# Hash-masked attention, rational feed-forward and mixture of experts in one kernel: one PSUM tile for a head's projection sums, the row-sum constant on GpSimd, and two weight conversions placed at the head of the feed-forward

## The chip, the cores and the metric

The kernel runs on one core of one Trainium2 chip. The metric is device time in microseconds (us), the median of several runs. Beside it one execution was profiled; its trace gives the rows shown below. Engines are named as in the trace: PE is TensorE's matmuls, PEld its weight loads, DVE is VectorE, ACT is ScalarE, POOL is GpSimd, SP is SyncE, which here only issues DMAs.

## The reference

Three layers follow one another. Only the first two are touched by the change.

```python
# attention: batch 2, 8 heads, 768 positions, head size 64, 6 hash bits
q_bits = (einsum('bhsd,dk->bhsk', q, proj) > 0)          # the same for k
mask   = q_bucket[:, :, :, None] == k_bucket[:, :, None, :]
scores = where(mask, q @ k.T / 8, -1e9);  scores -= scores.max(-1)
attn   = exp(scores);  attn = attn / (attn.sum(-1) + 1e-9);  x = attn @ v
# feed-forward on 1536 tokens of 512: w_in 512 x 2048, w_out 2048 x 512
h = x @ w_in
g = (a0 + a1*h + a2*h**2 + a3*h**3) / (1 + |b0|*|h| + |b1|*h**2 + 1e-6)
x = g @ w_out
# mixture of experts on the result: 8 experts, softmax gate with 8 rounds of balancing
```

The two feed-forward matrices come as 64-bit floats, everything else as 32-bit floats.

## The kernel before, in words

**Attention.** There are 16 heads. A head is worked in three groups of two 128-row tiles of queries, so the main loop runs over 48 groups (`it`), with lags: while group `it` gets its scores, group `it-2` is transposed and group `it-3` is multiplied with v. `scores` (L270 on) multiplies into a two-bank PSUM tile `s` of 768 columns; a DVE instruction (L285) copies it to the SBUF tile `e` and takes the row's minimum, and ACT (L286) writes the exponential over `e` and the row's sum into column 0 of a pair in `rse`, a tile whose column 1 was set to 1e-9 before the loop. `norm` reduces each pair with a DVE instruction (L291), takes the reciprocal on DVE (L292), and has POOL scale the two `e` tiles (L294). `trans` transposes `e` on PE (L308), ACT copies the high part (`pth`, L106) and DVE takes the low part (`ptl`, L109). `values` multiplies on PE (L323).

`prep_head_a` and `prep_head_b` make a head's operands two groups ahead of its use. `prep_head_b` (L251 on) multiplies q and k by the hash projection: for columns 0 to 511 and then 512 to 767 four matmuls sum into a PSUM bank `hp` (L259), and a DVE instruction (L260) thresholds each into `bits`; SP then issues two DMAs (L262, L263) that copy rows of `bits` into the score operands. PSUM's eight banks are four single banks (tag `b`: `tp`, `hp`, `pt`, `av`) and two two-bank tiles (tag `s`: `s`).

**Weights.** A 64-bit block of a feed-forward weight (128x512 values) is made into a high and a low 32-bit part by `prep_weights`, in five steps: an absolute value on ACT (L169) and a clamp on POOL (L170); four DVE instructions on the bits (L180 to L183); an add on POOL (L186), behind which the next raw block is loaded; a copy to the high part on ACT (L106, tile `wa` or `wb`); the low part on POOL (L103). Two tiles `c` are shared by all conversions. Eight blocks, 0 to 3 of w_in (`wa`) and of w_out (`wb`), are converted in the attention, each further one in the feed-forward, where the DVE steps write to a PSUM bank `bits`.

**Feed-forward.** Its steps run over 4 quarters of the hidden size, 3 tiles of 512 tokens and 4 blocks (48 steps). A step has 12 matmuls of the first product (`h`, L354), the rational function (ACT L372 to L374, POOL L375, DVE L376 and L377; one step later ACT L380 and L381, DVE L382 to L384; then ACT `gh` and POOL `gl`), and six steps later 12 matmuls of the second product (`acca`, L405).

**Order.** In the attention the order of the instructions on each engine is a planner's: it simulates the program with its own costs and takes ready work by its place in the program. It moves work far ahead: the eight conversions, written at groups 35 to 44, stand in the trace from 11 us on. In the feed-forward and behind it PE, ACT, DVE and POOL issue in the order in which the code is written; where the first of these instructions fall among those of the attention is the planner's too. Each engine runs its queue in order.

The lines around the change are L251 to L294 and the loop's `if it in wprep`; the feed-forward's loop begins with empty lists of conversions under way:

Of the kernel before, what the change touches and what calls it, by code (L numbers as in the profile page):

```python
# [14 lines left out]
F32 = mybir.dt.float32  # L15
# [5 lines left out]
AF = mybir.ActivationFunctionType  # L21
ALU = mybir.AluOpType
AX = mybir.AxisListType
# [3 lines left out]
QROW, KROW = 64, 96  # L27
# [8 lines left out]
def kernel(  # L36
# [16 lines left out]
    pe, act, dve, pool, sp = nc.tensor, nc.scalar, nc.vector, nc.gpsimd, nc.sync  # L53

    B, H, S, D = q.shape
    NB = proj.shape[1]
    DM, FF = moe_w_in.shape
    E, _, F2 = w1.shape
    P = 128
# [29 lines left out]
    def bank(name):  # L89
        return ps.tile([P, 512], F32, tag="b", bufs=4, name=name)  # L90

    def two_banks(name):
        return ps_s.tile([P, 2, 512], F32, tag="s", bufs=2, name=name)
# [19 lines left out]
    ap = qkv_pool_stack.enter_context(tc.tile_pool(name="attn", bufs=2))  # L113
# [137 lines left out]
    def prep_head_b(i):  # L251


        a1, a2, b1_, b2, _ = st[i]
        bits = ap.tile([P, S], F32R, tag="bits", bufs=1, name="bits")
        for n0, n1 in COLS:
            hp = bank("hp")[0:KROW + 2 * NB, 0:n1 - n0]
            for m, (j, r) in enumerate(((0, a1), (1, a1), (2, b1_), (3, b1_))):
                pe.matmul(hp, lhsT=pjr[:, j, 0:KROW + 2 * NB], rhs=r[:, n0:n1], start=m == 0, stop=m == 3)  # L259
            dve.tensor_scalar(bits[QROW:KROW + 2 * NB, n0:n1], hp[QROW:], thr[QROW:KROW + 2 * NB, 0:1],  # L260
                              thr[QROW:KROW + 2 * NB, 1:2], ALU.is_ge, ALU.mult)
        sp.dma_start(a2[QROW:QROW + 2 * NB].bitcast(F32), bits[QROW:QROW + 2 * NB].bitcast(F32))  # L262
        sp.dma_start(b2[QROW:QROW + 2 * NB].bitcast(F32), bits[KROW:KROW + 2 * NB].bitcast(F32))  # L263

    es = {}
    rsum_eps = [ap.tile([P, 2, 2], F32, tag=f"rse{n}", bufs=1, name="rse") for n in range(4)]
    for t in rsum_eps:
        dve.memset(t, 1e-9)

    def scores(gi, j):  # L270
        i, g = divmod(gi, G)
        a1, a2, b1_, b2, _ = st[i]
        t = 2 * g + j
        s = two_banks("s").rearrange("p a n -> p (a n)")
        cs = slice(t * P, (t + 1) * P)
        for n0, n1 in COLS:
            pe.matmul(s[:, n0:n1], lhsT=a1[:, cs], rhs=b1_[:, n0:n1], start=True, stop=False)
            pe.matmul(s[:, n0:n1], lhsT=a2[0:QROW + 2 * NB, cs], rhs=b2[0:QROW + 2 * NB, n0:n1],  # L278
                      start=False, stop=True)
        nm = ap.tile([P, 1], F32, tag="nm", bufs=4, name="nm")  # L280
        if j == 0:
            es[gi] = ([ap.tile([P, S], F32, tag="e", bufs=EB, name="e") for _ in range(2)],
                      rsum_eps[gi % len(rsum_eps)])
        e, rs = es[gi]
        dve.tensor_scalar(e[j], s[:, 0:S], BIG, None, ALU.min, ALU.min, accum_out=nm)  # L285
        act.activation(e[j], e[j], AF.Exp, bias=nm, scale=-1.0, accum_out=rs[:, j, 0:1])  # L286

    def norm(gi):
        e, rs_eps = es[gi]
        rs = ap.tile([P, 2], F32, tag="rs", bufs=4, name="rs")  # L290
        dve.tensor_reduce(rs, rs_eps, AX.X, ALU.add)  # L291
        dve.reciprocal(rs, rs)  # L292
        for j in range(2):
            pool.tensor_scalar(e[j], e[j], rs[:, j:j + 1], 0.0, ALU.mult, ALU.add)  # L294
# [403 lines left out]
    pjr = ap.tile([P, 4, P], F32R, tag="pjr", bufs=1, name="pjr")  # L698
# [8 lines left out]
    thr = const.tile([P, 2], F32, name="thr")  # L707
# [6 lines left out]
    dve.tensor_tensor(thr[:, 0:1], thr[:, 0:1], rowf[:, 2:3], ALU.add)  # L714

    prep_head_b(0)

    wprep = {NG - 13 + 3 * j: j for j in range(QF)}
    bits_in_psum = False
    for it in range(NG + VLAG):  # L720
        if it == CONST_AT:
            ca = const.tile([P, 4], F32, name="ca")
            cb = const.tile([P, 2], F32, name="cb")
            sp.dma_start(ca, moe_a.partition_broadcast(P))
            sp.dma_start(cb, moe_b.partition_broadcast(P))
            wg = const.tile([P, KC, E], F32, name="wg")
            sp.dma_start(wg, w_gate.rearrange("(c p) e -> p c e", p=P))
            wg2 = const.tile([P, KC, 2 * E], F32R, name="wg2")
            dve.tensor_copy(wg2[:, :, 0:E], wg)
            dve_lo(wg2[:, :, E:2 * E], wg, wg2[:, :, 0:E])  # L730

            ab = const.tile([P, 2], F32, name="ab")
            dve.tensor_scalar(ab, cb, -1.0, None, ALU.mult)
            dve.tensor_tensor(ab, ab, cb, ALU.max)
            na = const.tile([P, 4], F32, name="na")
            dve.tensor_scalar(na, ca, -1.0, None, ALU.mult)
            dbias = const.tile([P, 1], F32, name="dbias")
            dve.memset(dbias, 1.0 + 1e-6)
        if it == WLOAD:
            for c in range(2):  # L740
                load_weights(0, c)
                load_weights(1, c)
        i, g = divmod(it, G)
        ti, vi = it - TLAG, it - VLAG
        if it < NG:
            scores(it, 0)
        if i + 1 < len(heads) and g < 2:
            (prep_head_a, prep_head_b)[g](i + 1)
        if 0 <= ti < NG:
            trans(ti, 0)  # L750
        if 0 <= vi < NG:
            values(vi)
        if it < NG:
            scores(it, 1)
        if 0 <= ti < NG:
            trans(ti, 1)
            trans(ti, 2)
        if it < NG:
            norm(it)
        if it in wprep:  # L760
            for m in range(2):
                list(prep_weights(m, wprep[it]))
    qkv_pool_stack.close()

# [34 lines left out]
    def go(gen):  # L799

        return next(gen, 0) is None

    narrowing, acting, summing = [], [], []
    with tc.manual_schedule(engines={mybir.EngineType.PE, mybir.EngineType.Activation, mybir.EngineType.DVE,
                                     mybir.EngineType.Pool}):
        ws = None
        late, xs = None, [None] * 3
        for s in range(NS + QF):  # L810
            n = s - NS
            if n < 0:
                new = step_a(*divmod(s, QF))
            u, j = divmod(s - ALAG - QF, QF)
            summed = []
            if 0 <= u < NU - 1:
                gemm2_a(u, j)
                summed = [(u, j)]
            elif u == NU - 1:

                for j in range(3):
                    gemm2_a(u, j, range(QF - 1))
                for j in range(3):
                    gemm2_a(u, j, range(QF - 1, QF))
                summed = [(u, j) for j in range(3)]
            old_w = narrowing
            for w in old_w:
                go(w)
            for w in acting:
                go(w)  # L830
            if n < 0:
                go(new)
            narrowing = [prep_weights(m, i) for m, i in preps.get(s, ())]
            narrowing = [w for w in narrowing if go(w)]
            for w in old_w:
                go(w)
            for w in acting:
                go(w)
            for w in old_w:
                go(w)  # L840
            for w in narrowing:
                go(w)
            last = n >= 0 and summed[0][0] == NU - 1
            if last:
                gemm2_a(NU - 1, 3)
                for k in range(3):
                    go(xgen)
            for k in summed:
                sum_a(*k)
            if last:  # L850
                go(xgen)
                sum_a(NU - 1, 3)
                go(xgen)
                go(xgen)
            acting = [new] if n < 0 else []

            if s == NS - QS + ALAG + 1:
                def stemp():
                    c = [conv.tile([P, 512], F32, tag="c", name="c").rearrange("p (k c f) -> p k c f", k=2, c=2)
                         for _ in range(2)]  # L860
                    return c[0][:, 0], c[0][:, 1], c[1][:, 0]
                ws = w_blocks(0, stemp)
            if ws is not None and s < NS and not go(ws):
                if s == NS - 2:
                    wsec = w_second(0)
                go(wsec)
            if n == 0:
                x_stack.close()
                xs[0] = ffn_pool("x0", 1)
                xs[2] = ffn_pool("xt", 1)  # L870
                xgen = x_blocks(0)
                go(xgen)
            if last:
                break
# [77 lines left out]
```

## Time and profile before

| what | value |
|---|---|
| median of 3 runs | 1589.35 us (1587.63 to 1591.01) |
| profiled execution, whole | 1589.4 us |
| its span, first to last instruction | 1587.6 us |
| granted TensorE clock, mean | 0.994 |
| PE matmul busy | 1536.8 us (97%) |
| DVE busy | 1199.3 us (76%) |
| POOL busy | 938.9 us (59%) |
| ACT busy | 622.1 us (39%) |

The time of the whole is 1.8 us more than the span. In the trace the attention ends at about 291 us, the feed-forward at about 575 us, and the rest is the mixture of experts. The share of busy time of an engine is a mean over these stages, which have different limits.

### The profile page before, as it was taken

What the parts mean: (1) busy time and instruction counts of PE and PEld (TensorE: products, weight loads), DVE (VectorE), ACT (ScalarE), POOL (GpSimd) and SP (SyncE); (2) the same over time, 40 slices, a digit from 0 to 9 for tenths busy, and PEclk for the clock granted to TensorE, in tenths of its full rate; (3) what the DMA queues carried; (4) which work ended last, traced back from release to release, by engine and by line L of the source; (5) the groups of instructions that cost most, each with busy time, mean ns of one, the idle gap of its engine ahead of it and who ended that gap; (6) DMA issues with size and microseconds to landing.
All of it is one profiled execution on the core that took longest, in us unless ns stands there. A gap on an engine that the chain in (4) does not pass through costs nothing.

```text
span 1587.6 us, 22241 instructions
## 1 busy us (share of the span) xinstructions
PE 1536.8 (97%) x8071; PEld 1355.8 (85%) x8071; DVE 1199.3 (76%) x2116; ACT 622.1 (39%) x1167; POOL 938.9 (59%) x1165
## 2 busy tenths in 40 slices
PE   5989999899999999999999999999999999999999
PEld 4888889687777877889899999989899998989898
DVE  7989999799999984886666766676666666666665
ACT  4878888788777842111111111111111111111111
POOL 6777875577777976456644653564465356436530
PEclk8999999999999999999999999999999999999999
DMA  5322221021212000101010110101011001101002
GB/s 170 86 83 79 81 70 25 14 67 54 66 53 67 14 27 27 41 27 40 27 41 27 41 40 27 36 32 40 27 40 41 27 28 40 40 27 40 14 1 80
DMA packets 49406, 71.85 MB, mean 45 GB/s; under 512 B 4368, under 2 KB 35088, under 8 KB 49296
## 3 DMA queue, kind: packets, MB, share of 16 engines
q1 hardware_dynamic: 48432, 68.85, 14.1%
q8 instruction: 64, 1.05, 0.3%
q10 hardware_dynamic: 864, 1.57, 0.3%
q14 instruction: 46, 0.38, 0.1%
HBM read 59.79 MB, written 3.15 MB: 40 GB/s over the span
## 4 chain that ended last, share of the span: by engine, by line
PE 65%; DVE 2%; ACT 0%; issue 0%; DVEq 0%; ACTq 0%
PE accb L599 33%; PE prod L534 29%; PE acca L405 2%; PE h L354 1%; PE lp L635 0%; DVE t L470 0%; DVE t L473 0%; DVE c L559 0%; DVE part L417 0%; DVE gl L555 0%; ACT xb L106 0%; DVE t L480 0%; ACT gh L554 0%; DVE t L484 0%; DVE csum L676 0%
## 5 line engine op out<-in xcount | busy, mean ns | idle before, releaser
L534 PE MATMUL prod<-xb,ww 128*128 128x384 f32 x2688 | 481.7, 336 | 1.8 <-ACT m L106 1.3
L599 PE MATMUL accb<-wb,gh 128*128 128x512 f32 x1536 | 475.7, 391 | 2.9 <-ACT osum L106 2.5
L534 PEld LDWEIGHTS prod<-xb,ww 128*128 128x128 f32 x2688 | 469.8, 188 | 8.0 <-ACT m L106 1.6
L610 DVE SCALAR_TENSOR_TENSOR osum<-accb,gp,osum 128x512 f32<-128x512 f32 x336 | 251.7, 749 | 127.7 <-PE accb L599 126.0
L599 PEld LDWEIGHTS accb<-wb,gh 128*128 128x128 f32 x1536 | 287.0, 188 | 60.9 <-ACT osum L106 2.9
L599 PE MATMUL accb<-wb,gl 128*128 128x512 f32 x768 | 300.9, 392 | 0.4 <-DVE gl L555 0.4
L100 POOL TENSOR_SCALAR wb<-rb 128x512 fp32r<-128x512 f32 x64 | 40.2, 627 | 405.8 <-PE accb L599 405.8
L554 ACT ACTIVATE gh<-c 128x384 fp32r<-128x384 f32 x256 | 134.3, 526 | 352.5 <-DVE c L559 352.1
L106 ACT ACTIVATE m<-prod 128x384 f32<-128x384 f32 x64 | 31.5, 492 | 457.9 <-PE prod L534 457.9
L599 PEld LDWEIGHTS accb<-wb,gl 128*128 128x128 f32 x768 | 144.2, 188 | 32.0 <-DVE gl L555 1.7
L555 DVE SCALAR_TENSOR_TENSOR gl<-c,gh 128x384 fp32r<-128x384 f32 x256 | 165.2, 645 | 1.3 <-ACT gh L554 0.9
L559 DVE TENSOR_TENSOR c<-prod,u 128x384 f32<-128x384 f32 x192 | 106.6, 558 | 61.7 <-PE prod L534 54.1
L354 PE MATMUL h<-xh,wa 128*128 128x512 f32 x384 | 126.7, 392 | 3.4 <-DVE tu L377 3.4
L405 PE MATMUL acca<-gh,wb 128*128 128x512 f32 x384 | 126.4, 391 | 2.8 <-DVE part L417 1.7
L109 DVE TENSOR_TENSOR ptl<-pt,pth 128x512 fp32r<-128x512 f32 x144 | 94.5, 682 | 19.1 <-ACT pth L106 18.3
L559 DVE TENSOR_TENSOR c<-prod,m 128x384 f32<-128x384 f32 x64 | 35.7, 558 | 92.4 <-PE prod L534 92.4
L103 POOL TENSOR_TENSOR ww<-ra,ww 128x256 fp32r<-128x256 f32 x128 | 95.4, 746 | 10.7
L294 POOL TENSOR_SCALAR e<-e,rs 128x768 f32<-128x768 f32 x96 | 88.8, 937 | 20.8 <-DVE rs L292 11.3
L308 PE MATMUL pt<-idr,e 128*128 128x128 f32 x576 | 83.0, 279 | 11.1 <-DVE ptl L109 4.9
L285 DVE TENSOR_SCALAR_CACHE_REDUCE e<-s 128x768 f32<-128x768 f32 x96 | 90.9, 949 | 2.1 <-PE s L278 1.7
L286 ACT ACTIVATE e<-e,nm 128x768 f32<-128x768 f32 x96 | 89.9, 936 | 3.8 <-DVE e L285 3.1
L354 PEld LDWEIGHTS h<-xh,wa 128*128 128x128 f32 x384 | 72.1, 188 | 22.4 <-DVE tu L377 5.9
(168 smaller groups left out, 2546.3 us busy)
## 6 DMA issues: line engine op xcount, KB each, us to landing
ra<-in_moe_w_dram SPq DMA_DIRECT2D x32, 512.0 KB
rb<-in_moe_w_dram SPq DMA_DIRECT2D x32, 512.0 KB
ra<-in_moe_w_in_dram SPq DMA_DIRECT2D x16, 512.0 KB
rb<-in_moe_w_out_dram SPq DMA_DIRECT2D x16, 512.0 KB
qkv<-in_q_dram SPq DMA_DIRECT2D x16, 192.0 KB
qkv<-in_k_dram SPq DMA_DIRECT2D x16, 192.0 KB
qkv<-in_v_dram SPq DMA_DIRECT2D x16, 192.0 KB
a<-a SPq DMA_DIRECT2D x16, 192.0 KB
```

Source lines behind the costliest of these rows:

```text
L103: pool.tensor_tensor(lo, src, hi.bitcast(F32), ALU.subtract)
L109: dve.tensor_tensor(lo, src, hi.bitcast(F32), ALU.subtract)
L285: dve.tensor_scalar(e[j], s[:, 0:S], BIG, None, ALU.min, ALU.min, accum_out=nm)
L286: act.activation(e[j], e[j], AF.Exp, bias=nm, scale=-1.0, accum_out=rs[:, j, 0:1])
L354: pe.matmul(hps, lhsT=a[:, c], rhs=x[:, c], start=m == 0, stop=m == 3 * KC - 1)
L405: pe.matmul(o, lhsT=l[:, js], rhs=r, start=f == 0 and m == 0, stop=f == QF - 1 and m == 2)
L534: pe.matmul(o, lhsT=w[:, i, c], rhs=x[:, j, c], start=n == 0, stop=n == 5)
L554: act.activation(gh, c, AF.Relu)
L555: low.append(lambda: dve.scalar_tensor_tensor(gl, c, 0.0, gh.bitcast(F32), ALU.max, ALU.subtract))
L559: dve.tensor_tensor(c, o, x, ALU.add)
L599: pe.matmul(o, lhsT=l[:, ts], rhs=r, start=n == 0 and m == 0, stop=n == 1 and m == 2)
L610: dve.scalar_tensor_tensor(d, o, gate["p"][:, n, e:e + 1], d, ALU.mult, ALU.add)
```

## The change

The four single-bank accumulations of a head's projections become one two-bank tile of tag `s`, thresholded by one DVE instruction over 768 columns. The pairs with 1e-9 and the reduction over them go; POOL adds 1e-9 to the two row sums, and the reciprocal stays on DVE. Blocks 2 and 3 of w_out are no longer converted in the attention: their conversions are the first work written in the feed-forward's loop, with their first two steps ahead of step 0 and the others inside it.

```diff
         bits = ap.tile([P, S], F32R, tag="bits", bufs=1, name="bits")
+        rows = slice(QROW, KROW + 2 * NB)
+        hp = two_banks("hp").rearrange("p a n -> p (a n)")
         for n0, n1 in COLS:
-            hp = bank("hp")[0:KROW + 2 * NB, 0:n1 - n0]
             for m, (j, r) in enumerate(((0, a1), (1, a1), (2, b1_), (3, b1_))):
-                pe.matmul(hp, lhsT=pjr[:, j, 0:KROW + 2 * NB], rhs=r[:, n0:n1], start=m == 0, stop=m == 3)
-            dve.tensor_scalar(bits[QROW:KROW + 2 * NB, n0:n1], hp[QROW:], thr[QROW:KROW + 2 * NB, 0:1],
-                              thr[QROW:KROW + 2 * NB, 1:2], ALU.is_ge, ALU.mult)
+                pe.matmul(hp[0:KROW + 2 * NB, n0:n1], lhsT=pjr[:, j, 0:KROW + 2 * NB], rhs=r[:, n0:n1],
+                          start=m == 0, stop=m == 3)
+        dve.tensor_scalar(bits[rows], hp[rows, 0:S], thr[rows, 0:1], thr[rows, 1:2], ALU.is_ge, ALU.mult)
...
-    rsum_eps = [ap.tile([P, 2, 2], F32, tag=f"rse{n}", bufs=1, name="rse") for n in range(4)]
-    for t in rsum_eps:
-        dve.memset(t, 1e-9)
...
-                      rsum_eps[gi % len(rsum_eps)])
+                      ap.tile([P, 2], F32, tag="rsum", bufs=4, name="rsum"))
...
-        act.activation(e[j], e[j], AF.Exp, bias=nm, scale=-1.0, accum_out=rs[:, j, 0:1])
+        act.activation(e[j], e[j], AF.Exp, bias=nm, scale=-1.0, accum_out=rs[:, j:j + 1])
...
-        dve.tensor_reduce(rs, rs_eps, AX.X, ALU.add)
+        pool.tensor_scalar(rs, rsum, 1e-9, None, ALU.add)
         dve.reciprocal(rs, rs)
...
         if it in wprep:
-            for m in range(2):
+            for m in range(2 if wprep[it] < 2 else 1):
                 list(prep_weights(m, wprep[it]))
...
-    narrowing, acting, summing = [], [], []
+    narrowing, acting, summing = [prep_weights(1, i) for i in (2, 3)], [], []
...
+        for w in narrowing + narrowing:
+            go(w)
         for s in range(NS + QF):
```

## Rows read from the trace of the kernel before

**Rows 1.** Stretches of the run: length, then busy us (instructions) of each engine.
```profile
core 0: us, PE busy (x) PEld busy (x) DVE busy (x) ACT busy (x) POOL busy (x), PEclk, DMA share, GB/s
95.10:232.00 136.90, 127.38 (x930) 115.48 (x928) 124.11 (x271) 110.31 (x233) 108.71 (x133) 0.99 0.28 78
223.20:269.30 46.10, 45.95 (x349) 42.06 (x348) 42.06 (x96) 39.70 (x85) 31.84 (x43) 1.00 0.16 40
310.00:515.00 205.00, 195.64 (x838) 155.35 (x838) 193.95 (x291) 164.60 (x269) 155.88 (x141) 1.00 0.20 62
```
**Rows 2.** Waits from 223.2 to 269.3 us: total us, times, longest.
```profile
PEld pt L308 <- issue: 1.0, 3, 0.4
PEld pt L308 <- POOL e L294: 0.7, 2, 0.4
```
**Rows 3.** Order of time on SP: start, us; one such DMA ends each head's preparation.
```profile
95.10 0.75 SPq L263 DMA_DIRECT2D b<-bits  x1
...
166.84 0.76 SPq L263 DMA_DIRECT2D b<-bits  x1
...
231.99 0.76 SPq L263 DMA_DIRECT2D b<-bits  x1
...
262.66 0.77 SPq L263 DMA_DIRECT2D b<-bits  x1
```
**Rows 4.** Waits from 95.1 to 232 us.
```profile
ACT wa L106 <- POOL c L186: 5.0, 2, 2.5
ACT wb L106 <- POOL c L186: 4.8, 2, 2.5
```
**Rows 5.** Order of time at a conversion's end, with idle time before in brackets.
```profile
212.91 1.04 POOL L186 TENSOR_TENSOR c<-rb 128x512 f32<-128x512 f32 x1
...
213.98 0.63 ACT L106 ACTIVATE wb<-c 128x512 fp32r<-128x512 f32 x1 [2.29 <-POOL c L186]
...
217.79 0.31 PEld L308 LDWEIGHTS pt<-idr,e 128*128 128x128 f32 x3 [0.74 <-POOL e L294]
```
**Rows 6.** Instruction groups of DVE, 95.1 to 232 us: count, busy us, mean ns, idle before.
```profile
L260 DVE TENSOR_SCALAR bits<-hp,thr 44x512 fp32r<-44x512 f32 x8 | 6.6, 820 | 0.3
L260 DVE TENSOR_SCALAR bits<-hp,thr 44x256 fp32r<-44x256 f32 x8 | 4.4, 556 | 0.0
...
L291 DVE TENSOR_REDUCE rs<-rse 128x2 f32<-128x4 f32 x24 | 3.5, 148 | 0.5 <-ACT e L286 0.4
```
**Rows 7.** Order of time around a head's projections.
```profile
227.15 0.29 PEld L259 LDWEIGHTS hp<-a,pjr 128*108 128x108 f32 x2
...
228.44 0.08 DVE L285 DVE_READ_ACCUMULATOR e<-s 128x1 f32 x1
...
228.54 0.19 PEld L277 LDWEIGHTS s<-b,a 128*128 128x128 f32 x1
...
229.83 1.29 DVE L260 TENSOR_SCALAR bits<-hp,thr 44x512 fp32r<-44x512 f32 x2
```
**Rows 8.** Instruction groups of POOL: the smallest, and the smallest scaling.
```profile
L702 POOL IOTA row<- 128x1 int32 x1 | 0.1, 128 | 0.0
...
L100 POOL TENSOR_SCALAR xh<-xp 128x256 fp32r<-128x256 f32 x12 | 5.0, 420 | 5.4 <-DVE xp L334 5.4
```
**Rows 9.** Order of time at the attention's end and the feed-forward's start.
```profile
284.97 0.14 PEld L308 LDWEIGHTS pt<-idr,e 128*128 128x128 f32 x1 [1.32 <-POOL e L294]
...
291.64 0.74 POOL L103 TENSOR_TENSOR xl<-xp,xh 128x256 fp32r<-128x256 f32 x1
...
294.52 1.29 POOL L375 TENSOR_TENSOR tq<-tq,tw 128x512 f32<-128x512 f32 x1 [2.15 <-ACT tq L373]
295.14 0.69 DVE L376 TENSOR_TENSOR tu<-tu,h 128x512 f32<-128x512 f32 x1 [4.08 <-ACT tu L374]
295.85 0.69 ACT L380 ACTIVATE tr<-tq,dbias 128x512 f32<-128x512 f32 x1 [0.74 <-POOL tq L375]
```
**Rows 10.** Instruction groups of DVE, 310 to 515 us: one of a conversion's four steps.
```profile
L180 DVE TENSOR_SCALAR bits<-c 128x512 int32<-128x512 int32 x23 | 15.8, 689 | 0.0
```

More of the change, by code (lines that the diff above doesn't have):

```diff
@@ L282, in scores @@
             es[gi] = ([ap.tile([P, S], F32, tag="e", bufs=EB, name="e") for _ in range(2)],
-                      rsum_eps[gi % len(rsum_eps)])
+                      ap.tile([P, 2], F32, tag="rsum", bufs=4, name="rsum"))
         e, rs = es[gi]
         dve.tensor_scalar(e[j], s[:, 0:S], BIG, None, ALU.min, ALU.min, accum_out=nm)
-        act.activation(e[j], e[j], AF.Exp, bias=nm, scale=-1.0, accum_out=rs[:, j, 0:1])
+        act.activation(e[j], e[j], AF.Exp, bias=nm, scale=-1.0, accum_out=rs[:, j:j + 1])
     def norm(gi):
-        e, rs_eps = es[gi]
+        e, rsum = es[gi]
         rs = ap.tile([P, 2], F32, tag="rs", bufs=4, name="rs")
-        dve.tensor_reduce(rs, rs_eps, AX.X, ALU.add)
+        pool.tensor_scalar(rs, rsum, 1e-9, None, ALU.add)
         dve.reciprocal(rs, rs)
```

## The prediction

> **What bounds the kernel now.** I read the stretches of the run first, since each stage has another limit [rows 1]. From 223.2 to 269.3 us, three heads of attention without a weight conversion, PE is busy 45.95 of 46.10 us and DVE 42.06. From 95.1 to 232 us, heads with conversions among them, PE is busy only 127.38 of 136.90 while DVE has 124.11. In the feed-forward (310 to 515 us) DVE has 193.95 of 205 and PE 195.64: neither has room to catch up. The mixture of experts behind it is untouched.
>
> The second view is the order of time on SP: the last DMA of each head's preparation marks the heads [rows 3]. From 231.99 to 262.66 us two heads take 30.67 us, 15.34 each. From 95.10 to 231.99 eight heads take 136.89 us, 14.2 more than 8 x 15.34 = 122.7. The granted clock of 0.99 there [rows 1] explains about 1% of 136.9, 1.4 us; 12.8 us are left for the conversions that fall there, four whole ones and the end of a fifth.
>
> The third view, the waits of that stretch, says how a conversion costs this [rows 4]: ACT stood at the copy to `wa` or `wb` four times, 9.8 us in all, for POOL's add. ACT's queue is in order, so the copies of transposed tiles and the exponentials behind it wait too. One case in order of time [rows 5]: POOL adds at 212.91, ACT has waited 2.29 us when its copy starts at 213.98, and at 217.79, a scaling later, PE waits 0.74 us for POOL's `e`.
>
> **The change part by part.** All against the profiled execution: 1589.4 us, of which 1587.6 is its span; it equals the median of the runs, 1589.35, to 0.1 us.
>
> *Two conversions leave the attention.* By the ACT waits one costs 9.8 / 4 = 2.45 us [rows 4]. By the heads it is 12.8 / 4 = 3.2 at most, and by the last two alone, from 166.84 to 231.99 us (65.15 us for four heads, less 61.36), 1.9 [rows 3]. I take 2.45, the value in the middle: -4.9 us. The bounds are 0, if the planner, which sets this order anew, makes the remaining conversions stand as badly in the room that is left, and -6.4. Their absolute values and clamps need only raw data and a tile `c`, so the planner can still move them into gaps of the attention; no engine waits in order behind another for these, and I count them at nothing.
>
> *They stand at the head of the feed-forward.* There POOL has, in order, two adds (L186), then L375 of step 0; the second add needs all eight DVE steps. These take 0.689 us each in the feed-forward [rows 10], 5.5 us. DVE is free from 291.06 (L376 starts at 295.14 after 4.08 idle) [rows 9]. So if the front part was done earlier: DVE is through at 296.6, the second add (1.04, rows 5) ends at 297.6, L375 (1.29) at 298.9, where it ended at 295.81 before. ACT's L380 of step 0 follows it [rows 9]: +3.1 us. DVE's idle 4.08 us hide most of the eight steps; what shows is their end and the adds in POOL's queue. The delay stays, since the next steps hang on the same chain and the 205 us behind it are 95% full on both engines [rows 1]. If the planner lets nothing start before the attention's last POOL work ends at 292.38 (291.64 + 0.74), a clamp comes ahead (estimate 0.7 us, between the 0.42 for 256 columns in rows 8 and the 1.04 of the add in rows 5), so DVE starts at 293.1, 2.0 later: +5.1. If the DVE steps fit into the last microseconds of the attention, 0. The loads of blocks 4 and 5 of w_out move with the adds, to about 297 us, off SP's queue in the attention; that queue is free then. They are first needed at step 6; six steps of 12 matmuls lie between: covered.
>
> *One threshold instruction.* 820 + 556 ns become, with the slope (820 - 556) / 256 = 1.03 ns a column, 820 + 264 = 1084 ns: 0.29 us of DVE a head [rows 6]. With the reduction, 3 x 0.148 us a head, DVE gets 0.74 us a head back. Beside a PE that is busy 99.7% [rows 1] I cost this at nothing.
>
> *Two banks from the scores.* `hp` now takes one of the two score tiles from its first weight load at 227.15 to the threshold's end, 229.83 + 1.29 = 231.12: 4.0 us [rows 7]. The score that began at 228.54 would need the other tile, whose reading ended at 228.52: it just fits. So there is no stall with this order; if DVE is late by some tenths, the score waits as long. Queued behind a late score on PE are transposes and v products, which the planner may put first. Bounds 0 and 0.5 us x 16 heads = +8; I take +0.5, near the row that shows a fit.
>
> *The add on POOL.* The trace has no POOL add of two columns. Below it stands the 0.128 us of a one-column instruction, above it 0.420 for 256 columns [rows 8]; I take 0.2. POOL is busy 31.84 of 46.10 us [rows 1], so its time is covered. What is new is a wait: DVE's reciprocal now waits for POOL, and behind it on DVE stand score reads and `ptl`, for which PE waits. With two groups between scaling and transposing this is hidden, except at the attention's end, where PE waits 1.32 us for the scaling [rows 9]: the longer chain adds 0.2 and a hand-over, +0.3. Bounds 0 and the +8 of the third rival.
>
> Sum: -4.9 + 3.1 + 0.5 + 0.3 = -1.0, so 1588.4 us.
>
> **A rule weighed.** The waits of PE in the stretch without conversions are 1.0 + 0.7 = 1.7 us of 46.10 in their two largest groups [rows 2], and PEld is busy 42.06 [rows 1]. The Trainium skill's page "Perfetto Trace Analysis", section "Identifying the Most-Contended Engine", says that the matmuls' busy share is no good measure of PE's headroom and the weight loads' busy share is. By it PE has 9% left there where the matmul row shows 0.3%, and the DVE relief would pay. By the matmul row the relief is worth 0, by the rule something up to those waits; this is the first rival.
>
> **The rivals.**
> First, faster: the DVE relief pays. PE's waits of 1.7 us in three heads [rows 2] are 0.57 us a head; over some 15 heads 8.5 us, of which the relief of 0.74 us a head might take half: -4.3 more, 1584.1 us. For it: 0.7 us of them stand behind POOL's scaling, which waits for DVE's reciprocal. Against it: the larger part is put down to no wait, and 0.3% idle matmul time leaves no place for it.
>
> Second, slower: nothing is won in the attention. The planner's new order lets the six conversions left, or a late score, cost what the eight did; then 3.1 + 0.5 + 0.3 stay: 1593.3 us. It decides once the attention's end comes less than 0.7 us earlier. For it: these stalls come from an order planned with costs that the chip does not keep. Against it: each of the four ACT waits belongs to one conversion.
>
> Third, slower: DVE waits for POOL. In a head without conversions DVE has (46.10 - 42.06) / 3 = 1.35 us idle, with the 0.74 won 2.1, or 0.7 for each of its three pairs. If the reciprocal waits longer than that for a POOL that is in a scaling, DVE becomes the bound; 0.85 us a pair would add 0.15 x 48 = 7 us: 1595.6 us. For it: POOL's queue is in order too. Against it: the planner sees the dependency and can put the reciprocal later.
>
> Fourth, the two conversions do not leave: the planner, free to place the first feed-forward work, moves most of it back into the attention. Then little changes: 1589.5 us.
>
> **How the numbers follow.** The forecast has 0.40 (its own range 1585 to 1592), the first rival 0.28, the second 0.16, the third 0.10, the fourth 0.06. A measurement of this kernel tells about 0.2% from no change, 3.2 us. Faster by more: 0.28 and 0.06 from the forecast's lower end, 0.34. Slower: 0.16 + 0.10, and 0.01 of the forecast, 0.27. Within: 0.39. The range reaches from beyond the first rival to the third, 1581 to 1596 us.
>
> **What would show it.** ACT's waits for POOL's add in the attention fall by about two, and the last third of the heads runs at 15.3 us. The attention ends 3 to 5 us earlier; L380 of step 0 then starts 8 us after the last `xp`, where it was 5. If heads without conversions take less than 15.2 us, the first rival holds; if they take 15.8 or more with DVE idle before L292, the third; with PE idle before the scores, the shared tiles cost. An attention that ends as late as before would make the forecast wrong.

## The result and the profile after

The changed kernel takes 1606.67 us (median of 5 runs, 1605.96 to 1607.88), against 1589.75 us for the kernel before in the same comparison: ratio 1.0107, 95% interval 1.0093 to 1.0122. It is 17 us slower; the forecast was 1588.4 us with a range up to 1596. The profiled span went from 1587.6 to 1604.3 us, 16.7 more. The last `xp` (the sum of a head's two value halves on DVE, which ends the attention) starts at 304.14 us where it was 290.64, 13.5 later, and the first ACT L380 of the feed-forward (now L378) at 312.64, where it was 295.85 [rows 9]: 16.8 later. In the kernel before and in the changed kernel:

```profile
290.64 0.42 DVE L334 TENSOR_TENSOR xp<-av,avt 64x256 f32<-64x256 f32 x1 [1.01 <-ACT avt L106]
```

```profile
304.14 0.42 DVE L332 TENSOR_TENSOR xp<-av,avt 64x256 f32<-64x256 f32 x1 [1.01 <-ACT avt L106]
...
312.64 0.69 ACT L378 ACTIVATE tr<-tq,dbias 128x512 f32<-128x512 f32 x1 [0.62 <-POOL tq L373]
```

So the loss is in the attention, with 3.3 us more at the head of the feed-forward, and what follows takes as long as before. The profiled execution of a later run, `e6_dve_add`, took 5368.6 us against some 1589 in its other nine, so that run is judged by its times alone.

The stretches again, four heads of attention without a conversion (length, then busy us of each engine):

```profile
core 0: us, PE busy (x) PEld busy (x) DVE busy (x) ACT busy (x) POOL busy (x), PEclk, DMA share, GB/s
171.77:239.76 67.99, 65.60 (x465) 57.77 (x464) 54.97 (x113) 53.22 (x112) 48.82 (x73) 1.00 0.24 64
```

They answer to the second row of [rows 1]: there PE was busy 45.95 of 46.10 us (99.7%), here 65.60 of 67.99 (96.5%), at a granted clock of 1.00 in both. DVE went from 91% to 81%: it has less to do, and yet the heads take longer. The heads, by the DMA that ends each preparation (start, us):

```profile
173.71 0.77 SPq L264 DMA_DIRECT2D b<-bits  x1
191.28 0.77 SPq L264 DMA_DIRECT2D b<-bits  x1
207.70 0.77 SPq L264 DMA_DIRECT2D b<-bits  x1
225.27 0.77 SPq L264 DMA_DIRECT2D b<-bits  x1
241.70 0.77 SPq L264 DMA_DIRECT2D b<-bits  x1
```

Heads alternate between 17.6 and 16.4 us, 17.0 on average, where heads without conversions took 15.34 [rows 3]. The waits of the same stretch (total us, times, longest):

```profile
DVE rs L290 <- POOL rs L289: 7.5, 10, 2.5
POOL rs L289 <- ACT e L284: 7.4, 6, 2.4
ACT e L284 <- DVE e L283: 7.0, 10, 2.2
```

None of the first two kinds could exist before: DVE now stands at the reciprocal for POOL's add, and POOL stands at the add for ACT's row sum. From 60 to 290 us:

```profile
POOL rs L289 <- ACT e L284: 25.7, 20, 2.4
DVE rs L290 <- POOL rs L289: 25.6, 33, 2.7
PEld pt L306 <- POOL e L292: 2.5, 4, 0.7
```

Seven of the 33 waits of DVE are longer than 1.6 us and make 16.4 of the 25.6 us. One of the long cases in order of time, with the idle time before an instruction in brackets:

```profile
213.49 1.28 DVE L109 TENSOR_TENSOR ptl<-pt,pth 128x512 fp32r<-128x512 f32 x2
...
214.52 0.18 ACT L284 ACTIVATION_READ_ACCUMULATOR e<-e,nm 128x1 f32 x1
...
215.34 0.50 POOL L100 TENSOR_SCALAR sq<-qkv 128x384 fp32r<-128x384 f32 x1
...
215.93 1.01 POOL L103 TENSOR_TENSOR sq<-qkv,sq 128x384 fp32r<-128x384 f32 x1
...
217.03 0.21 POOL L289 TENSOR_SCALAR rs<-rsum 128x2 f32<-128x2 f32 x1
217.27 0.17 DVE L290 RECIPROCAL rs<-rs 128x2 f32<-128x2 f32 x1 [2.50 <-POOL rs L289]
217.37 0.96 DVE L283 TENSOR_SCALAR_CACHE_REDUCE e<-s 128x768 f32<-128x768 f32 x1
...
218.39 0.19 PEld L275 LDWEIGHTS s<-b,a 128*128 128x128 f32 x1 [0.36 <-DVE e L283]
218.43 0.94 ACT L284 ACTIVATE e<-e,nm 128x768 f32<-128x768 f32 x1 [2.22 <-POOL e L292]
```

DVE is free at 214.77, and ACT has made the row sum by 214.70 (214.52 + 0.18). DVE's next instruction is the reciprocal, and POOL's add, which could have run then, stands behind the split of the next head's q. DVE waits 2.50 us for an instruction of 0.21. Behind the reciprocal stands the reading of a score tile; ACT's exponential has waited 2.22 us when it starts and PE's next score 0.36 for the tile.

The planner also orders DVE otherwise than before. From 60 to 290 us, 33 of the 40 reciprocals in the changed kernel's trace stand directly ahead of a score reading; before it was 4 of 42, and 28 stood directly behind one. So a wait at the reciprocal now falls on the score readings.

### The profile page after: what moved, and what is told of

Its sections match the earlier page's. It is cut to its first block, busy times and chain, and to the rows that moved or that the text cites. A ratio compares the mean times of both kernels' runs of the same rounds, so it can differ in the third digit from the quotient of the medians.

```text
span 1604.3 us, 22263 instructions
## 1 busy us (share of the span) xinstructions
PE 1549.2 (97%) x8071; PEld 1360.1 (85%) x8071; DVE 1193.6 (74%) x2048; ACT 624.3 (39%) x1167; POOL 948.0 (59%) x1213
## 4 chain that ended last, share of the span: by engine, by line
PE 64%; DVE 2%; ACT 0%; issue 0%; DVEq 0%; ACTq 0%
PE accb L597 32%; PE prod L532 28%; PE acca L403 2%; PE h L352 1%; PE lp L633 0%; DVE t L468 0%; DVE t L471 0%; DVE c L557 0%; DVE part L415 0%; DVE gl L553 0%; ACT xb L106 0%; DVE t L478 0%; ACT gh L552 0%; DVE t L482 0%; DVE csum L674 0%
## 5 line engine op out<-in xcount | busy, mean ns | idle before, releaser
L403 PEld LDWEIGHTS acca<-gh,wb 128*128 128x128 f32 x384 | 72.1, 188 | 20.3 <-DVE part L415 2.5
```

Of the source, the lines that this page charges most:

```text
L403: pe.matmul(o, lhsT=l[:, js], rhs=r, start=f == 0 and m == 0, stop=f == QF - 1 and m == 2)
```

## The experiments

The theories: **A**, DVE's in-order queue stands at the reciprocal for POOL's add, which is late because of what POOL does before it (the third rival); **B**, the two-bank tile takes a score tile and PE waits; **C**, any new order of the planner costs this; **D**, the chain from the exponential to the scaling is longer, on whatever engine; **E**, POOL's own time and queue. Ratios are to the kernel before, measured beside each.

**One part at a time.** `e1_two_bank` has only the first hunk of the diff, `e2_pool_add` only the row-sum hunks, `e3_conv_moved` only the last three; `e4_no_pool_add` is the changed kernel without the row-sum hunks.

> Only the one two-bank tile for a head's projections. Theory A (DVE's reciprocal waits for GpSimd's add): no add here, so within 3 us of the kernel before, heads without conversions at 15.3 to 15.5 us. Theory B (the two-bank tile takes a score tile and PE waits for the next): 8 to 15 us slower, heads without conversions at 16.5 to 17 us.

Measured: 1594.47 us, 1.0039 (1.0024 to 1.0054), 6 us slower. Its late heads alternate between 15.2 and 16.2 us. Neither theory's number. B's wait hardly shows in the trace: from 60 to 290 us the weight loads of the scores waited 0.6 us for DVE's reading, where it was 0.2 before. What makes the 6 us was not found.

> Only the 1e-9 added by GpSimd. Theory A: 8 to 15 us slower, heads without conversions near 17 us, DVE waiting for L289's counterpart at the reciprocal some 2 us a head. Theory B: within 3 us of the kernel before.

Measured: 1609.97 us, 1.0138 (1.0123 to 1.0153), 21.7 us slower, more than the whole change and more than A had expected. The last four heads alternate between 17.9 and 15.4 us, 16.6 on average. The waits from 60 to 290 us:

```profile
DVE rs L289 <- POOL rs L288: 30.8, 26, 2.8
POOL rs L288 <- ACT e L283: 27.3, 11, 4.6
```

> Only the two conversions moved. The attention ends about 5 us earlier, the feed-forward's first steps lose 2 to 3 us: 1 to 4 us faster than the kernel before under theory A and B alike. If the new order of the planner alone costs the time (theory C), this one is slower by 5 us or more too.

Measured: 1587.16 us, 0.9992 (0.9983 to 1.0002). No difference that can be measured; C falls as a general cause: this new order costs nothing. Inside it the two terms show. The attention's last `xp` starts at 287.08 us, 3.6 earlier than before, and from the tenth head on heads take 15.2 to 15.4 us. The head of the feed-forward:

```profile
287.08 0.42 DVE L334 TENSOR_TENSOR xp<-av,avt 64x256 f32<-64x256 f32 x1 [1.01 <-ACT avt L106]
287.42 0.67 DVE L180 TENSOR_SCALAR bits<-c 128x512 int32<-128x512 int32 x1
...
292.48 0.69 DVE L183 SCALAR_TENSOR_TENSOR rb<-rb,bits 128x512 f32<-128x512 uint32 x1
...
293.25 1.04 POOL L186 TENSOR_TENSOR c<-rb 128x512 f32<-128x512 f32 x1 [1.86 <-DVE rb L183]
...
294.25 1.30 POOL L375 TENSOR_TENSOR tq<-tq,tw 128x512 f32<-128x512 f32 x1
...
295.58 0.69 ACT L380 ACTIVATE tr<-tq,dbias 128x512 f32<-128x512 f32 x1 [0.63 <-POOL tq L375]
```

L380 comes 8.50 us after the last `xp`; before it was 295.85 - 290.64 = 5.21. Of the 3.6 us 3.3 are given back.

> The changed kernel with the row sums reduced with 1e-9 on DVE as before. Theory A: 12 us or more faster than the changed kernel, that is within 4 us of the kernel before. Theory B: no more than 4 us faster than the changed kernel, some 12 us slower than the kernel before.

Measured: 1587.67 us, 0.9994 (0.9985 to 1.0004): as the kernel before, and 18 to 19 us faster than the changed kernel (by the ratios and by the times, which come from two comparisons). The add on POOL, with the order that the planner makes for it, is the loss.

**Which property of the add.** In the next four the rest is as in the changed kernel.

```diff
-        pool.tensor_scalar(rs, rsum, 1e-9, None, ALU.add)
+        dve.tensor_scalar(rs, rsum, 1e-9, None, ALU.add)                # e6
+        act.activation(rs, rsum, AF.Identity, bias=eps)                 # e9, eps a [P, 1] tile of 1e-9
# e7: the add stays; reciprocal and scaling in a function called after scores(it + 1, 1)
# e8: reduction with 1e-9 on DVE as before, and beside it
+        pool.tensor_scalar(zs, rs_eps[:, :, 0], 0.0, None, ALU.mult)    # zs: the scaling's second scalar
```

> The changed kernel, the add of 1e-9 on DVE in place of GpSimd. Theory A (DVE stands at the reciprocal for GpSimd's add): within 3 us of 1587.7, the kernel without the GpSimd add, since DVE then waits for ACT alone. Theory D (the longer chain of two instructions between the exponential and the scaling, on whatever engine): near the changed kernel, 1600 us or more.

Measured: 1589.21 us, 1.0009 (0.9999 to 1.0018). D falls, for DVE; that DVE then waits for ACT alone is not shown, since no trace of this run is read.

> The changed kernel, with GpSimd's add where it was but the reciprocal and the scaling written one group later, behind that group's second scores. Theory A: DVE finds the sum ready, its wait before the reciprocal falls from some 30 us to under 8, and the time to 1588 to 1595. Theory D: the chain gets longer still, no faster than 1606. Theory E (GpSimd's own time for the 48 adds): 1606, unchanged.

Measured: 1621.6 us, 1.0215 (1.02 to 1.023). Theory A expected the opposite and missed: writing the reciprocal later does not place it where the sum is ready. The waits from 60 to 290 us are fewer and longer:

```profile
POOL rs L289 <- ACT e L284: 19.0, 4, 4.7
DVE rs L296 <- POOL rs L289: 18.5, 11, 3.7
PE s L275 <- DVE e L283: 11.2, 9, 3.5
```

DVE waits 7 us less for POOL than in the changed kernel, and the time is 15 us longer; PE's scores wait 11.2 us for DVE's reading, where the changed kernel has 0.2. So the sum of DVE's waits does not measure the loss, and A alone does not explain this run. Only D had named "no faster than 1606".

> The changed kernel with the row sums reduced with 1e-9 on DVE as before, and GpSimd still doing one two-column instruction on the row sums a group (it makes zeros, which the scaling adds), so that DVE waits for no GpSimd result. Theory A: within 4 us of 1587.7. Theory E: as slow as the changed kernel, 1600 or more.

Measured: 1594.78 us, 1.0048 (1.0032 to 1.0065). Neither A's nor E's number: with DVE's reciprocal free of it, POOL's instruction still costs 7 to 9 us against the kernel without it, and 9 to 12 us less than the add. The waits from 60 to 290 us:

```profile
POOL zs L295 <- ACT e L287: 22.0, 14, 2.5
DVE e L286 <- POOL zs L295: 7.1, 4, 1.8
```

The split is rough. DVE is not wholly free of POOL's instruction: four score readings wait for it, and why they do was not found. And the scaling with two pointers is longer, 0.998 us against 0.940 in the changed kernel over that stretch.

> The changed kernel, the add of 1e-9 on ACT, which has just made the row sum. Theory A, if it is the work queued on GpSimd that DVE waits for: ACT adds in its own order behind the exponential, DVE waits little, 1588 to 1596 us (ACT has 48 instructions of about 0.2 us more). If any hand-over through a second engine costs it: 1600 or more.

Measured: 1584.35 us, 0.9978 (0.9969 to 0.9988), faster than both kernels and below A's range. The chain has as many instructions as with POOL, and ACT's is even longer than POOL's (0.213 us for most), but DVE hardly waits at the reciprocal (60 to 290 us: count, busy us, mean ns, idle before):

```profile
L291 ACT ACTIVATE rs<-rsum,eps 128x2 f32<-128x2 f32 x41 | 11.9, 291 | 0.2
L292 DVE RECIPROCAL rs<-rs 128x2 f32<-128x2 f32 x42 | 6.5, 156 | 0.6 <-ACT rs L291 0.6
```

With this D falls altogether. But the engine is not all that differs: 17 of the 42 reciprocals stand directly ahead of a score reading here and 28 directly behind one, against 33 and 6 of 40 in the changed kernel. So how much of the difference comes from the engine and how much from DVE's order stays open.

**The same without the two-bank tile.** `e5_no_two_bank` is the changed kernel without its first hunk; `e12_pool_op_alone_no_wait` the kernel before with the instruction of e8; `e11_act_add_alone` the kernel before with the add on ACT; `e10_act_add_no_two_bank` that with the conversions moved.

> The changed kernel with the projections' sums in two single banks as before: GpSimd's add and the moved conversions are left. Theory A (DVE stands for GpSimd's add, whatever the tile): 1603 to 1612 us, DVE waiting 20 us or more before the reciprocal. If it is the two together (the shared tile held longer because the threshold stands behind the waiting reciprocal): 1595 us or less.

Measured: 1611.27 us, 1.0148 (1.0133 to 1.0163). DVE waits 30.5 us at the reciprocal, as A had it; the tile is not needed for the loss.

> The kernel before, plus one two-column GpSimd instruction a group on the row sums whose result only GpSimd reads. Theory A: of the 21.7 us of the add alone, GpSimd's own queue (its time and its standing for the exponential) makes a third or less, so 1590 to 1596 us; the rest needs DVE's wait. Theory E (GpSimd's time and queue are all of it): 1605 or more.

Measured: 1595.26 us, 1.0048 (1.0033 to 1.0063): 7.4 us of the 21.7, about a third, as A had it. Here DVE waits 0.3 us for POOL's instruction; the longer scaling (0.986 us against 0.908 for most, 96 of them) is in the 7.4.

> The kernel before with the add of 1e-9 on ACT, nothing else changed. Theory A: no GpSimd in the hand-over, so 1584 to 1592 us, against 1610 with the add on GpSimd.

Measured: 1586.93 us, 0.9992 (0.9983 to 1.0002). As A had it.

> The add on ACT and the two conversions moved, the projections in single banks. If the two-bank tile gives part of the 3.6 us by which the same kernel with it beats the one before: 1586 to 1589 us. If it costs as it did alone (6 us): 1580 to 1583.

Measured: 1585.71 us, 0.9986 (0.9976 to 0.9995). Between the two ranges. Beside e9's 0.9978 the intervals overlap; in this company the two-bank tile shows no cost.

**What stands ahead of the add.** Two runs take the low part of q's split (1.01 us) off POOL:

```diff
-            hi, lo = (dve.tensor_copy, dve_lo) if i == 0 and j < 2 else (pool_hi, pool_lo)
+            hi, lo = (dve.tensor_copy, dve_lo) if i == 0 and j < 2 else (pool_hi, dve_lo if j == 0 else pool_lo)
```

> The changed kernel with the low part of a head's q, a GpSimd instruction of 1.01 us that stands ahead of the add in the longest waits, done by DVE. Theory A (DVE waits for what is queued on GpSimd ahead of the add): the waits of 2.5 us go, DVE's wait before the reciprocal falls below 18 us from 25.6, and the time lies at least 4 us nearer to the next kernel's than the changed kernel lies to the one without the add (under 15 us apart instead of 19). If the waits keep their length, what stands ahead on GpSimd is not their cause.

Measured: 1595.73 us, 1.0043 (1.0028 to 1.0058), 10 to 11 us faster than the changed kernel although DVE does more; all three signs that A had named came. The waits from 60 to 290 us:

```profile
DVE rs L290 <- POOL rs L289: 17.3, 32, 1.4
POOL rs L289 <- ACT e L284: 34.4, 21, 3.3
```

> The same move in the kernel without the GpSimd add: what the move itself costs. DVE has 16 instructions of about 0.6 us more and is not the bound in heads without conversions: 1587 to 1593 us.

Measured: 1584.69 us, 0.998 (0.9969 to 0.9991), faster than expected. The add costs 10 to 11 us here, where it cost 18 to 19; the longest wait went from 2.7 to 1.4 us. So in the long waits what is queued on POOL ahead of the add is what DVE waits for, and shortening it gave back some 8 us. DVE's order did not do this: in e13 37 of the 42 reciprocals stand directly ahead of a score reading, more than in the changed kernel. The rest is not all of this kind: 26 of the 32 waits are 0.2 to 0.6 us, 9 us together as in the changed kernel, most of them 0.26 or 0.41 and so not far above the add's own 0.21, and POOL stands at the add 34.4 us for ACT.

## Why the prediction was wrong

**The step that failed** is the add on POOL. I put it at +0.3 us, hidden "with two groups between scaling and transposing". It costs 18 to 19 us (ratio 1.0107 against e4's 0.9994, 1606.67 against 1587.67 us). The two groups do cover the chain from scaling to transposing: PE's weight loads for the transposes wait 2.5 us for POOL's scaling from 60 to 290 us, where it was 12.0 before. They do not cover the queue behind the reciprocal: DVE's score reads and `ptl` have no such lag, and they stand behind an instruction that waits for POOL. I named that queue and then priced only the chain.

**The third rival** had the mechanism, with a chance of 0.10 and a price of +7 us, and the sign that I had named for it came: heads of 15.8 us or more (17.0) with DVE idle before the reciprocal. Its price was wrong in two ways. It took one wait for every pair and set DVE's mean idle time against it; the waits are mostly 0.26 to 0.4 us with one of 2.5 every second head in the stretch without conversions, and idle time that is spread over a head does not absorb a long one. And it left POOL out: POOL's queue is in order as well, so an add placed ahead of its row sum stops the scalings and splits behind it (25.7 us in the changed kernel). By e12, whose instruction stands 12.8 us for ACT, that side alone is some 7 us. "The planner sees the dependency and can put the reciprocal later" was no argument: it put the reciprocal ahead of the score readings, where before it stood behind them, and e7, with the reciprocal written later, is slower still. Why the planner places them so was not tried.

**Two conversions out of the attention**, forecast -4.9: 3.6 us in e3's trace, by the last `xp`. The mechanism is there: ACT's waits for the add fall from 5 to 3 between 60 and 290 us in e3, and the late heads run at 15.3 us. That is 1.8 us each, near the 1.9 of the last two conversions. But the profiled execution of e3 was its slowest, 1590.27 us; its median is 1.1 us under that of the kernel before, which with the 3.3 us below makes 4.4, or 2.2 each. So the term was right in kind, and in size a tenth to a third too large.

**Their place at the head of the feed-forward**, forecast +3.1: 8.50 - 5.21 = 3.3 us in e3, and 312.64 - 304.14 = 8.50 in the changed kernel too. The planner had moved the front steps ahead, as assumed: between the last `xp` and L380 POOL does the two adds and no clamp; DVE starts on the bits at 287.42 us, right behind the last `xp`, and the second add in POOL's queue sets L375.

**The threshold and the two-bank tile.** One instruction takes 1.085 us, as worked out (1084 ns). The tile's +0.5 us fits beside the moved conversions (e4 against e3, 0.9994 and 0.9992); alone it costs 6 us, inside its bounds. Why the same tile costs nothing in one order and 6 us in the other stays open.

**The first rival** falls. The kernel with the whole relief of DVE and no add on POOL is e9 (e4 has the one threshold alone), and its late heads take 15.1 and 15.6 us in turn, 15.34 on average, as before:

```profile
222.99 0.77 SPq L264 DMA_DIRECT2D b<-bits  x1
238.58 0.77 SPq L264 DMA_DIRECT2D b<-bits  x1
253.67 0.77 SPq L264 DMA_DIRECT2D b<-bits  x1
```

That e9's 1584.35 us lies beside this rival's 1584.1 is chance, since its heads without conversions gained nothing. So PE had no headroom there that this relief could use, and the busy row of the matmuls described the stretch better than the weight loads, which were busy 91% [rows 1]. The Trainium skill's page "Perfetto Trace Analysis" (section "Identifying the Most-Contended Engine") would judge the headroom by the weight loads or by the share of peak FLOPs; the second was not worked out here. The second rival (nothing won in the attention) and the fourth did not happen: e3's attention ends 3.6 us earlier, and the two conversions run behind it.

## What to carry over

Before moving a small instruction to another engine, ask what stands in that engine's queue ahead of it and what stands behind the instruction that will wait for it; its own 0.2 us is not the price. In this kernel the add cost nothing on ACT, which had made the operand a moment ago, and 18 to 19 us on POOL, which was in the middle of other work; the planner's order of DVE changed with it, and the two were not told apart. Spare time in the mean (DVE had 9% here) did not pay for waits that come in pieces of 2.5 us.

## What was not expected

The hand-over itself is short in the case shown: the reciprocal starts 0.03 us after POOL's add ends (217.03 + 0.21, then 217.27), so little of that wait of 2.50 us is signalling. A two-column instruction takes 0.21 us on POOL, 0.29 on ACT and 0.15 to 0.17 on DVE, and ACT, the slowest of the three at it, was a better place for it than POOL.
